# A start-up change in a one-core attention-plus-MLP kernel: constant idle products, V units split in two, earlier wk transposes, tile 0 transposed on TensorE

## Chip, cores, metric

The kernel runs on one core of a Trainium2 chip. The metric is the device time of one execution in microseconds (us). Single executions spread by about 1 us here, so medians, ranges and ratios over several runs are given, always with runs of the kernel before on the same chip.

## The reference, cut to what matters

```python
def reference(A_x, A_wqkv, A_w_phi, A_wo, B_x, B_w1, B_w3, B_w2):
    # x: 1 x 2048 x 640 bf16; 32 heads of 20; MLP width 1536
    xn = _layernorm(x)
    # A: q, k, v = xn @ wqkv; per head phi(q), phi(k) = softmaxes of +-(. @ w_phi);
    #    linear attention with kv = phi(k)^T v and z = sum phi(k); then @ wo
    # B: (silu(xn @ w1) * (xn @ w3)) @ w2
    return x + A(xn) + B(xn)
```

Three facts matter. Everything needs the normalised tokens transposed (xnT). V of the first 512 tokens is computed from centred tokens (xcT), with the scale applied at the eviction, so that it can start early. The feature matrix is folded into the key weights ("fold1": Wkp = wk @ w_phi, block by block). That needs wk transposed, which the DMA does while loading.

## The kernel before

The program lists operations with their dependencies. A planner at build time orders them per engine with estimated durations and seeded random tie-breaking. Then waits are put in. Where TensorE has nothing to do in the first 12 us, the planner inserts idle products ("filler"), which keep the array active. The parts that the change touches:

```python
memset("DVE", zero[:], 0.0, 9)                       # operand of the idle products
...
def filler(t, until):
    while t < until:
        cold = t < 5.2
        n = 512 if until - t > 0.5 else 128
        c = n / (1200 if cold else 2400)
        # emits matmul(bank, zero[:, 0:128], zero[:, 0:n])
        P.all.pop().raw = set(zeroed)                # waits for the memset
...
def v_pair(t, level):        # V0 and V1 in one unit of four PSUM banks
    both = P.begin(4, level, stream="V")
    for a, b, u in ((0, 3, 0), (0, 3, 1), (3, DC, 0), (3, DC, 1)):
        ...                  # chunks 0-2 of V0, of V1, then chunks 3-4 of each
...
load_x(0, 1, lv); ...; on_act(2.65, load_x, 3, 4)    # token tiles 0..3
load_w13(0, 384, lv - 4)                             # w1, w3: columns for 3 MLP units
first = [P.all[n]]                                   # the first of these two loads
for e in range(DC):
    o = load_wT(1, e, lv - 9 - e, first)             # transposes of wk wait for it
...
TURNED = (0,)                                        # tile 0 of xnT by DMA transpose
```

An "MLP unit" is five products of 128x512 with w1 and five with w3. Only three such units can run on the first weight loads.

The softmax here doesn't subtract the row's maximum and nothing guards it: scores larger than these inputs give would overflow.

## Time and profile before

| | before |
|---|---|
| median of the first 3 runs | 274.41 us (274.11 to 274.45) |
| span of the profiled run | 272.6 us |
| TensorE busy | 268.8 us, 99% |
| idle products | 4.84 us of the chain |
| first MLP weight load / first fold weight load | 14.01 / 20.40 us |

In the chain of waits a line has its start, its length and what ran. In a timeline a line has start, length, engine, operation and count, with the idle time ahead of it and its releaser in square brackets. PE is TensorE and PEld its weight loads, DVE VectorE, ACT ScalarE, POOL GpSimd; SPq and ACTq are the queues of SyncE and ScalarE, from which loads are issued. Ends of products are modelled, so I use starts and the spacing of starts.

### The profile page before, as it was taken

What the parts mean: (1) busy time and instruction counts of PE and PEld (TensorE: products, weight loads), DVE (VectorE), ACT (ScalarE), POOL (GpSimd) and SP (SyncE); (2) the same over time, 40 slices, a digit from 0 to 9 for tenths busy, and PEclk for the clock granted to TensorE, in tenths of its full rate; (3) what the DMA queues carried; (4) which work ended last, traced back from release to release, by engine and by line L of the source; (5) the groups of instructions that cost most, each with busy time, mean ns of one, the idle gap of its engine ahead of it and who ended that gap; (6) DMA issues with size and microseconds to landing.
All of it is one profiled execution on the core that took longest, in us unless ns stands there. A gap on an engine that the chain in (4) does not pass through costs nothing.

```text
span 272.6 us, 5091 instructions
## 1 busy us (share of the span) xinstructions
PE 268.8 (99%) x2099; PEld 159.9 (59%) x2099; DVE 183.8 (67%) x326; ACT 104.2 (38%) x193; POOL 60.5 (22%) x101
## 2 busy tenths in 40 slices
PE   8999999999999999999999999999999999999996
PEld 4747446777754448444444446677677774444774
DVE  5748998999999443588969795677673215666112
ACT  5637754776754540356663354100110002222000
POOL 3320552689999900000000000000000000000000
PEclk9999999999999999999999999999999999999999
DMA  7968996763000000803111111433353222000001
GB/s 233 183 95 258 345 216 129 118 175 114 2 0 2 0 0 10 284 1 46 29 26 24 24 26 25 98 100 96 90 107 83 64 75 72 0 0 0 26 24 48
DMA packets 41959, 22.14 MB, mean 81 GB/s; under 512 B 27728, under 2 KB 41936, under 8 KB 41936
## 3 DMA queue, kind: packets, MB, share of 16 engines
q1 hardware_dynamic: 41360, 21.17, 32.6%
q10 hardware_dynamic: 576, 0.66, 0.7%
q8 instruction: 16, 0.26, 0.4%
q14 instruction: 7, 0.06, 0.1%
HBM read 12.81 MB, written 2.62 MB: 57 GB/s over the span
## 4 chain that ended last, share of the span: by engine, by line
PE 99%; DVE 0%; issue 0%
PE PS L620 96%; PE PS L1094 2%; PE PS L811 1%; PE PS L865 0%; DVE xres L628 0%; DVE zero L628 0%; DVE warm L628 0%
## 5 line engine op out<-in xcount | busy, mean ns | idle before, releaser
L620 PE MATMUL PS<-xnT,w_s 128*128 128x512 bf16 x480 | 106.7, 379 | 0.0
L620 PEld LDWEIGHTS PS<-xnT,w_s 128*128 128x128 bf16 x480 | 46.6, 98 | 55.2
L620 PE MATMUL PS<-w_s,hT 128*128 128x320 bf16 (+2 forms) x384 | 55.0, 300 | 0.0
L628 ACT ACTIVATE th<-PS 128x512 f32<-128x512 f32 x48 | 28.7, 597 | 68.8 <-PE PS L620 68.8
L628 DVE SCALAR_TENSOR_TENSOR t<-th,PS 128x512 bf16<-128x512 f32 x48 | 32.7, 684 | 29.8 <-ACT th L628 29.8
L620 PEld LDWEIGHTS PS<-w_s,hT 128*128 128x128 bf16 x384 | 36.9, 98 | 14.8
L628 POOL TENSOR_TENSOR ekt<-ekt,rS 128x640 bf16<-128x640 bf16 x32 | 39.4, 1268 | 0.7 <-DVE rS L628 0.7
L628 DVE TENSOR_TENSOR xres<-PS,xres 128x640 bf16<-128x640 f32 (+2 forms) x17 | 13.4, 786 | 36.9 <-PE PS L620 36.9
L628 DVE SCALAR_TENSOR_TENSOR hT<-t,PS 128x512 bf16<-128x512 bf16 x48 | 32.7, 683 | 1.3
L628 ACT ACTIVATE EqT<-PS 128x512 bf16<-128x512 f32 x40 | 21.8, 594 | 11.3 <-PE PS L620 11.3
L628 ACT ACTIVATE e_s<-PS 128x64 f32<-128x64 f32 x32 | 9.1, 283 | 40.6 <-PE PS L620 40.1
L620 PE MATMUL PS<-wo_s,oT 128*128 128x320 bf16 (+2 forms) x160 | 24.5, 299 | 0.0
L628 DVE TENSOR_TENSOR prod<-PS,g_s 128x1280 bf16<-128x1280 f32 x16 | 23.9, 1492 | 0.6
L620 PE MATMUL PS<-Wkp,xnT 128*128 128x320 bf16 x160 | 23.9, 299 | 0.0
L628 ACT ACTIVATE ekt<-PS 128x640 bf16<-128x640 f32 x32 | 20.7, 698 | 7.5 <-PE PS L620 7.3
L620 PE MATMUL PS<-xnT,Wqp 128*128 128x512 bf16 x100 | 23.4, 380 | 0.0
L628 DVE TENSOR_REDUCE S<-ekt 128x64 f32<-128x1280 bf16 x16 | 22.9, 1449 | 0.0
L620 PEld LDWEIGHTS PS<-wo_s,oT 128*128 128x128 bf16 x160 | 15.7, 98 | 6.1
L620 PEld LDWEIGHTS PS<-Wkp,xnT 128*128 128x128 bf16 x160 | 15.5, 98 | 5.9
L620 PE MATMUL PS<-wv,xnT 128*128 128x320 bf16 x120 | 18.3, 299 | 0.0
L628 DVE BATCH_NORM_STATS2 bst<-x_tok 128x6 f32<-128x320 bf16 x32 | 13.9, 464 | 2.9 <-DMA x_tok<-in_A_x_dram 2.9
L620 PEld LDWEIGHTS PS<-xnT,Wqp 128*128 128x128 bf16 x100 | 9.3, 98 | 10.8
(68 smaller groups left out, 171.0 us busy)
## 6 DMA issues: line engine op xcount, KB each, us to landing
w_s<-in_B_w_dram SPq DMA_DIRECT2D x8, 480.0 KB, 7.7
xres<-in_A_x_dram SPq DMA_DIRECT2D x16, 160.0 KB, 2.2
out_dram<-xres SPq DMA_DIRECT2D x15, 160.0 KB, 1.8
x_tok<-in_A_x_dram SPq DMA_DIRECT2D x3, 640.0 KB, 7.5
w_s<-in_B_w_dram SPq DMA_DIRECT2D x1, 1920.0 KB, 9.1
wo_s<-in_A_wo_dram SPq DMA_DIRECT2D x1, 800.0 KB, 4.7
x_tok<-in_A_x_dram SPq DMA_DIRECT2D x2, 160.0 KB, 3.4
x_tok<-in_A_x_dram ACTq DMA_DIRECT2D x2, 160.0 KB, 3.8
```

Of the source, the lines that this page charges most:

```text
L620: return nc.tensor.matmul(o(u.k), l, r, start=start, stop=stop, skip_group_check=shared)
L628: return getattr(e, name)(*[at(a, u) for a in args], **{k: at(v, u) for k, v in kw.items()})
L811: return nc.tensor.transpose(PSb[:, a:a + 128], l, ident[:])
L1094: return nc.tensor.matmul(bank(u.k, n), zero[:, 0:128], zero[:, 0:n], start=True, stop=True)
```

## The change

It is meant to shorten the start: no memset and no wait ahead of the idle products, less of them, V0 able to start without tile 1, wk transposed sooner, and one DMA transpose less on the queue.

```diff
-TURNED = (0,)
-SEED = 385
+TURNED = ()
+SEED = 817
...
-        memset("DVE", zero[:], 0.0, 9)
-        zeroed.append(P.all[-1])
...
-    def v_pair(t, level):
+    def v_split(t, level, later, cut):
+        u = P.begin(2, level)                      # chunks 0..2
+        ...
+                P.begin(0, later).name = f"V{t}b"  # chunks 3..4, same banks, later
+                P.unit.anchor = u
...
+    ones = nc.const_aps.tensor(1.0, [128, 512], bf)
...
-            n = 512 if until - t > 0.5 else 128
-            c = n / (1200 if cold else 2400)
+            n = 512 if until - t > 0.9 else 128
+            c = n / (1200 if t < 6.5 else 2400)
...
-                return nc.tensor.matmul(bank(u.k, n), zero[:, 0:128], zero[:, 0:n], ...)
+                return nc.tensor.matmul(bank(u.k, n), ones[:, 0:128], ones[:, 0:n], ...)
...
-    on_act(2.65, load_x, 3, 4)
+    third = on_act(2.65, load_x, 3, 4)
...
-    first = [P.all[n]]
+    first = [third]
...
-    v_pair(0, 6e4)
+    v_split(0, 6e4 + 20, 6e4 - 8, 3)
+    v_split(1, 6e4 - 5, 6e4 - 9, 3)
...
-    P.schedule({"PE": 1.25, ...}, filler, 12.0, SEED, 175.0)
+    P.schedule({"PE": 0.8, ...}, filler, 12.0, SEED, 175.0)
```

More of the change, by code (lines that the diff above doesn't have):

```diff
@@ L573, in bass_parallel_sum__linear_kernel_hedgehog__glu_gated_swiglu__prompt_kernel @@
     hT1 = new("hT1", [128, FC, 512], bf, RH + 12288)
-    zero = new("zero", [128, 512], bf, RH + 12288)
     RE = region(40960)
@@ L723, in load_wT @@
                     A_wqkv[:, which * D + 128 * e:which * D + 128 * e + 128], level, True, after)
-    zeroed = []
     def consts():
         memset("DVE", warm[:], 0.0, 19)
-        memset("DVE", zero[:], 0.0, 9)
-        zeroed.append(P.all[-1])
         add([w_act(warm[:], warm[:], ACT.Exp, 8)], [warm[:]], [warm[:]], None, 3e9)
@@ L791, in centre @@
         o, i, z = xc[:, t, :], x_tok[:, t, :], mv[:, t, 6:7]
-        if by == "ACT":
-            add([way("ACT", "activation", (junk[:], i, ACT.Copy), dict(scale=-1.0 / D, accum_out=z), 0.86, 0.92)],
+        if by == "BOTH":
+            h, zb = D // 2, mv[:, t, 7:8]
+            add([way("ACT", "activation", (junk[:, 0:h], i[:, 0:h], ACT.Copy), dict(scale=-1.0 / D, accum_out=z),
+                     0.55, 0.58)], [junk[:, 0:h], z], [i[:, 0:h]], None, level)
+            add([way("DVE", "tensor_scalar", (junk[:, h:D], i[:, h:D], -1.0 / D, None, ALU.mult, ALU.add),
+                     dict(accum_out=zb), 0.48, 0.52)], [junk[:, h:D], zb], [i[:, h:D]], None, level)
+            add([w_op("DVE", "tensor_scalar", (o, i, z, zb, ALU.add, ALU.add), 0.31, 0.41)], [o], [i, z, zb], None,
+                level)
+        elif by == "ACT":
+            add([way("ACT", "activation", (junk[:], i, ACT.Copy), dict(scale=-1.0 / D, accum_out=z), 0.86, 0.87)],
                 [junk[:], z], [i], None, level)
-            add([w_op("DVE", "tensor_scalar", (o, i, z, None, ALU.add), 0.35, 0.44),
+            add([w_op("DVE", "tensor_scalar", (o, i, z, None, ALU.add), 0.31, 0.41),
                  w_act(o, i, ACT.Identity, D, 1.0, z)], [o], [i, z], None, level)
@@ L798, in centre @@
             m = mv[:, t, 0:1]
-            add([w_op("DVE", "tensor_scalar", (o, i, m, None, ALU.subtract), 0.35, 0.44)], [o], [i, m], None, level)
+            add([w_op("DVE", "tensor_scalar", (o, i, m, None, ALU.subtract), 0.31, 0.41)], [o], [i, m], None, level)
     def xc_transpose(t, level):
@@ L831, in v_first, with src @@
             [v2[:, t, 0:672]], [r], [0, 1], 1e6)
-    def v_pair(t, level):
-        both = P.begin(4, level, stream="V")
-        both.name = f"V{t}+"
-        for a, b, u in ((0, 3, 0), (0, 3, 1), (3, DC, 0), (3, DC, 1)):
-            if b == DC and u == 1:
-                P.begin(0, level - 30, stream="V").name = f"V{t + 1}"
-                P.unit.anchor = both
+    def v_split(t, level, later, cut):
+        u = P.begin(2, level)
+        u.name = f"V{t}a"
+        for a, b in ((0, cut), (cut, DC)):
+            if a:
+                P.begin(0, later).name = f"V{t}b"
+                P.unit.anchor = u
             for i in range(a, b):
                 for q in range(2):
-                    mm(2 * u + q, lambda k, q=q, u=u: bank(k + 2 * u + q, 320), xcT[:, t + u, i, :],
-                       wv[:, i, 320 * q:320 * q + 320], i == 0, i == DC - 1)
-            if b == DC:
-                o = v2[:, t + u, 0:672].rearrange("p (b h c) -> p b h c", b=2, c=21)[:, :, :, 0:DH]
-                r = mv[:, t + u, 4:5]
-                def src(k, u=u):
-                    return bank2(k + 2 * u, 320).rearrange("p b (h c) -> p b h c", c=DH)
-                last = P.unit.mms[-1]
-                P.unit = both
-                add([w_act(o, src, ACT.Copy, D, r),
-                     w_op("DVE", "tensor_scalar", (o, src, r, None, ALU.mult), 0.74, 0.83)],
-                    [v2[:, t + u, 0:672]], [r], [2 * u, 2 * u + 1], 1e6, [last])
+                    mm(q, lambda k, q=q: bank(k + q, 320), xcT[:, t, i, :], wv[:, i, 320 * q:320 * q + 320],
+                       i == 0, i == DC - 1)
+        P.unit.mms[0].war.add(u.mms[-1])
+        o = v2[:, t, 0:672].rearrange("p (b h c) -> p b h c", b=2, c=21)[:, :, :, 0:DH]
+        r = mv[:, t, 4:5]
+        def src(k):
+            return bank2(k, 320).rearrange("p b (h c) -> p b h c", c=DH)
+        last = P.unit.mms[-1]
+        P.unit = u
+        add([w_act(o, src, ACT.Copy, D, r), w_op("DVE", "tensor_scalar", (o, src, r, None, ALU.mult), 0.74, 0.83)],
+            [v2[:, t, 0:672]], [r], [0, 1], 1e6, [last])
     def xn_transpose(t, level):
@@ L1089, in filler @@
         while t < until:
-            cold = t < 5.2
-            n = 512 if until - t > 0.5 else 128
-            c = n / (1200 if cold else 2400)
+            n = 512 if until - t > 0.9 else 128
+            c = n / (1200 if t < 6.5 else 2400)
             def emit(n=n):
-                return nc.tensor.matmul(bank(u.k, n), zero[:, 0:128], zero[:, 0:n], start=True, stop=True)
+                return nc.tensor.matmul(bank(u.k, n), ones[:, 0:128], ones[:, 0:n], start=True, stop=True)
             P.mm(emit, [], 0, c, n)
-            P.all.pop().raw = set(zeroed)
+            P.all.pop()
             t += c
@@ L1209, in bass_parallel_sum__linear_kernel_hedgehog__glu_gated_swiglu__prompt_kernel @@
         out_tile(t, when(200 + 5 * t))
-    P.schedule({"PE": 1.25, "ACT": 1.12, "DVE": 0.93, "POOL": 0.8, "SP": 0.81}, filler, 12.0, SEED, 175.0)
+    P.schedule({"PE": 0.8, "ACT": 1.12, "DVE": 0.93, "POOL": 0.8, "SP": 0.81}, filler, 12.0, SEED, 175.0)
     lists = P.emit(finish)
```

## The prediction

> **What bounds the kernel now.** I read the page first: busy shares, slices, and the chain that ended last.
>
> ```profile
> PE 268.8 (99%) x2099; PEld 159.9 (59%) x2099; DVE 183.8 (67%) x326; ACT 104.2 (38%) x193; POOL 60.5 (22%) x101
> ...
> PE   8999999999999999999999999999999999999996
> ...
> PE 99%; DVE 0%; issue 0%
> PE PS L620 96%; PE PS L1094 2%; PE PS L811 1%; PE PS L865 0%; DVE xres L628 0%; DVE zero L628 0%; DVE warm L628 0%
> ```
>
> TensorE has no hole between the first slice and the last, and the chain is TensorE for 99% of the span. The next engine, VectorE, is at 67%. So a change to loads, evictions or their order pays only where TensorE does something other than work of the reference: the idle products (line 1094), which fill its waits at the start, and products run before its clock is up. The chain in order of time (start, length, what) says how much that is:
>
> ```profile
> 0.96 0.28 DVE zero L628
> ...
> 1.29 3.60 PE PS L1094 x11
> 4.88 0.54 PE PS L811 x5
> 5.42 0.74 PE PS L1094 x4
> 6.16 0.53 PE PS L811 x5
> 6.70 2.45 PE PS L620 x16
> 9.15 0.28 PE PS L811 x5
> 9.43 0.54 PE PS L620 x4
> 9.97 0.50 PE PS L1094 x9
> 10.47 1.36 PE PS L620 x10
> 11.83 0.28 PE PS L811 x5
> 12.11 0.84 PE PS L865 x15
> 12.95 119.14 PE PS L620 x945
> ...
> 270.13 0.42 DVE xres L628
> ```
>
> Idle products take 3.60 + 0.74 + 0.50 = 4.84 us. The last real product ends at 270.13, so the useful stream is 270.13 - 1.29 - 4.84 = 264.00 us, and after 12.95 us nothing but useful products is left (two pieces of 0.01 us apart). Five transposes take 0.54 and 0.53 us early on and 0.28 later; sixteen value products take 2.45 us where ten take 1.36 later, which would be 2.18. The slow clock therefore costs 0.26 + 0.25 + 0.27 = 0.78 us of useful work. Everything a perfect start could give back is the 1.24 us of idle products after 4.88, this 0.78, and what the arrival of token tile 0 allows before that (0.2 us at most, below).
>
> The view of the tile of idle operands and that of the normalised-token transposes show the clock in single durations (ns, min/median/max), the view of VectorE's timeline when tile 0 is centred, and TensorE's waits that nothing but the start makes it wait:
>
> ```profile
> L1094 PE MATMUL PS<-zero x24: 219/314/634, 1.3 to 10.3; 128*128 128x128 bf16 x16, 128*128 128x512 bf16 x8
> ```
> ```profile
> 4.03 0.39 DVE L628 TENSOR_SCALAR xc<-x_tok,mv 128x640 bf16<-128x640 bf16 x1
> ...
> 4.89 0.39 DVE L628 TENSOR_SCALAR xc<-x_tok,mv 128x640 bf16<-128x640 bf16 x1
> ```
> ```profile
> PE PS L1094 <- DVE zero L628: 1.3, 1, 1.3
> ```
>
> A 128x128 product lasts 314 ns cold and 219 warm. Tile 0 is centred at 4.42 and its transposes start at 4.68; tile 1 at 5.28, but its transposes start only at 5.96, behind idle products that were issued for a later arrival than came.
>
> **What the Trainium skill says.** "TensorE: Matmul & The Clock Gate", Part 1 (the HAM clock gate): the array starts at half clock, and one window of about 3.4 us of sustained activity, free-running against the kernel, releases it. The trace agrees on the two rates: from start to start the idle 128x512 products are 427 ns apart until the change and products of that width 216 ns apart later. The change falls at about 7.1 us, inside the value products (267 ns apart, one of 193, then 136), 5.8 us after the first product. The page's PEclk row shows 1.00 from the start and hides it. Same page, Part 4 (PE-mode transpose): a transpose lasts some 275 ns in a kernel; here the median over the first twenty is 267 ns, but their spacing is 56 ns warm, which is what counts in a stream. "Perfetto Trace Analysis", Identifying the Most-Contended Engine: matmul busy time is a poor measure of distance to the roofline. That warning holds for single durations (379 ns against 216 ns of spacing), so I count with pieces of the chain instead. "DMA: Bandwidth & Descriptors", Issuing engines are not separate DMA queues: all queues share the 16 engines. The trace fits: the two weight loads issued at 4.68 and 5.11 land at 10.66 and 12.16, and the transpose of tile 0, issued behind them at 6.52, at 12.88.
>
> **The change part by part.**
> (1) Idle products from a constant. The zero tile (a 0.27 us memset on VectorE, and TensorE's wait for it until 1.29) goes. The constant is written by 0.47 us, before the common start, so idle products can begin at about 0.85. This moves no useful product: tile 0 lands at 3.15, the sum on ScalarE and the centring end at 4.42. It gives the clock 0.44 us more of activity. If its release follows the first product, it comes at 6.7 instead of 7.1, and 0.44 us less useful work runs at half rate: -0.2. If the window's edges stand where they are, nothing. I take -0.1.
> (2) The idle stretches are cut anew (wide ones only above 0.9 us, half rate assumed until 6.5 us, costs of centring lowered to what is measured). First transposes at about 4.5 for 4.68: -0.15. Between tile 0's and tile 1's transposes, data allow 5.35: of the 0.74 us of idle products about 0.3 stay: -0.45.
> (3) V0 and V1 in two units each instead of one four-bank unit. The product count is the same (20 + 20). V0's first three chunks need only tile 0, so they can run from about 5.9, when its transpose is evicted (5.94 before), instead of 6.49. By then a few more useful products run cold: +0.1. V0's last two chunks need the weights landing at about 7.0. Summed in order: V0a 5.9 to 7.3, V1a to 8.1, V0b and V1b to 9.2.
> (4) Tile 0's normalised tokens transposed on TensorE: five more transposes, 0.28 us by the row above, and one more eviction of 0.49 us on VectorE or 0.70 on ScalarE. They are ready at about 6.5 (normalised by 6.49) and fit where 0.50 us of idle products stood at 9.97: they replace idle time rather than add to it. Of the 0.50 I leave 0.2 standing, since tile 2 is not centred before 8.58 and must still be transposed and evicted: -0.30 +0.28. On the queue it frees 1.31 us of issue.
> (5) Transposes of wk behind tile 3 (landing at 7.28) rather than the first weight load (10.66): issued about 3.4 us earlier, so the folded key weights come some 3 us before 20.6, and the token loads behind them at about 17 instead of 20.5. TensorE has MLP work throughout, so this is worth nothing in the sum; it only gives slack.
> (6) The new seed reorders units up to 175 us. The work is equal and there is no gap to win. Switches into and out of the row mode cost about 0.1 us each and their number is fixed by the sixteen query tiles. I take 0 +- 0.2.
>
> Sum: -0.1 -0.15 -0.45 +0.1 -0.30 +0.28 = -0.62 us. From 274.41 this is 273.8.
>
> **The rivals.**
> A: the clock decides. Over 0.31 to 3.73 (one window back from the two edges that the change at 7.14 implies) TensorE was busy from 1.29, 71%; from 0.85 it would be 84%. If that suffices, the clock is up at 3.73, no useful product is cold, and 0.78 us more goes: about 273.0. Against: that window is not full, and the edges may stand elsewhere in each run; the spread of three runs (274.11 to 274.45) is the size of such a shift.
> B: a new wait in place of the filler. With idle products cut short, tile 2's centring (8.19 to 8.58, after ScalarE's sum) or the weights at 7.0 to 7.3 would hold V2 at 10.3 just the same; the idle time moves, and the five transposes are added in full: 274.3 to 274.6. For: ScalarE handles tile 2's sum only at 7.33. Against: tile 2 landed near 5.05, so the order can be better.
> C: the earlier wk transposes hold back the weight loads needed by the first MLP unit at 14.14. Ring order puts them behind, and the loads land at 12.16 before, so 1 to 1.5 us of delay would be needed to hurt: up to +1, unlikely.
> D: the new order opens a stall in the middle (VectorE is 80% busy or more in slices 4 to 13). Each tenth of a slice is 0.7 us; nothing in the diff adds more than one eviction, so I give over 1 us one chance in fifteen.
>
> **Range and chances.** The centre of the sum is 273.8; A weighs more than C and D together, so I put 273.7. Low end: most of A, 273.0. High end: B, 274.5. Two per cent is 5.5 us. Only 4.84 us of idle products plus 0.78 us of slow clock exist, and 3.6 of that lie before tile 0 can be there, so faster by 2% cannot come from this stage: 0.01. Slower needs a 5.5 us stall on an engine now never waiting: 0.01. Within 2%: 0.98.
>
> **What would show it.** Idle products from about 0.85, still until about 4.5 (1 right); fewer than 0.8 us of them after 4.6 (2, 4); tile 1's transposes before 5.6 and value products before 6.2 (2, 3); twenty normalised-token transposes; first MLP product near 13.5 for 14.14; wk transposes issued at 7.3 to 7.8 (5). From there on the stream should be the old one moved by 0.5 to 0.8 us, ending near 269.5 for 270.13. Wrong if TensorE shows a wait after 13 us, if the first MLP product waits for a weight load, if the clock comes up more than 1 us away from 7, or if the gain at 13 us is gone again at 175.

## The result, and the profile after

A ratio is the mean time of one kernel's runs over that of the other's of the same rounds, so it is not quite the ratio of the medians quoted.

| rounds | changed, median (range) | before, median (range) | ratio, 95% interval |
|---|---|---|---|
| first | 274.21 (273.51 to 274.48), 6 runs | 274.32 (273.46 to 274.52), 6 runs | 0.9998, 0.9981 to 1.0016 |
| with e5, another chip | 273.74 (273.52 to 274.45), 6 runs | 274.85 (273.54 to 276.07), 11 runs | 0.9969, 0.9941 to 0.9997 |
| with e10, another chip | 273.93 (273.23 to 274.66), 6 runs | 274.25 (273.61 to 275.58), 11 runs | 0.9979, 0.9958 to 0.9999 |

The differences of the means are -0.05, -0.81 and -0.50 us, -0.45 us on average, for the -0.62 us of the prediction's sum. It is the same within 2%, as predicted. The first rounds alone show no gain at all. The page of the changed kernel, busy shares and the engines of the chain:

```profile
PE 267.5 (98%) x2082; PEld 159.9 (59%) x2101; DVE 180.8 (66%) x322; ACT 106.0 (39%) x197; POOL 61.1 (22%) x101
...
PE 92%; DMA 3%; SPq 3%; issue 1%; ACTq 0%; ACT 0%; DVE 0%
```

Two things are to be seen. There are 2101 weight loads but 2082 matmuls: 19 records of matmuls are missing. Each leaves a hole of one product (216 ns for 128x512), and "0.05 issue" in the chain below is such a hole and no wait. Before comparing busy times of two traces, compare these two counts. What is real is that the chain no longer is all TensorE. In order of time:

```profile
2.36 4.85 DMA x_tok<-in_A_x_dram
...
7.22 1.22 SPq L693
...
8.49 2.37 SPq L693
...
15.22 3.49 DMA wqkT<-in_A_wqkv_dram
18.71 0.14 issue
18.85 9.07 PE PS L619 x75
27.92 0.05 issue
```

The end now hangs on the load of token tile 3, the transposes of wk issued behind it (line 693) and the landing of the last one at 18.71. At that instant TensorE stands in the first fold, as the timeline shows:

```profile
18.05 0.42 PE L619 MATMUL PS<-BDc,wqkT 128*128 128x140 bf16 x5
...
18.85 0.85 PE L619 MATMUL PS<-BDc,wqkT 128*128 128x140 bf16 x13 [0.38 <-DMA wqkT<-in_A_wqkv_dram]
```

The fifth product starts at 18.25 and the sixth at 18.85 where 0.06 is usual: a wait of 0.54 us. (The brackets say 0.38 because the end of the fifth is modelled.) The kernel before ran thirty MLP products ahead of the folds and went through them without a wait:

```profile
20.62 1.82 PE L620 MATMUL PS<-BDc,wqkT 128*128 128x140 bf16 x30
```

The changed kernel runs only twenty first. Its head start is there: the first MLP weight load is at 13.61 for 14.01, 0.40 us earlier. Then the fold wait takes 0.54 away, other differences of the plan give 0.16 back, and the last product starts at 269.81 for 269.83. The start itself, by TensorE's timeline of the changed kernel:

```profile
0.84 4.00 PE L1098 MATMUL PS<-const-bfloat16-1.0 128*128 128x512 bf16 x15 [0.84 <-PEq L1263]
...
4.63 0.74 PE L814 MATMUL PS<-ident,xc 128*128 128x128 bf16 x5
...
5.17 0.84 PE L1098 MATMUL PS<-const-bfloat16-1.0 128*128 128x128 bf16 x6
...
5.96 1.23 PE L619 MATMUL PS<-wv,xcT 128*128 128x320 bf16 x6
```

Idle products from 0.85, first value products at 5.96 for 6.49, idle products and waits of 0.79 us after the first transposes, and a wait of 0.14 at 8.1 us, for 1.25 together.

### The profile page after: what moved, and what is told of

The parts are those of the page before. It is cut to its first block, busy times and chain, and to the rows that moved or that the text cites. A ratio compares the mean times of both kernels' runs of the same rounds, so it can differ in the third digit from the quotient of the medians.

```text
span 272.6 us, 5074 instructions
## 1 busy us (share of the span) xinstructions
PE 267.5 (98%) x2082; PEld 159.9 (59%) x2101; DVE 180.8 (66%) x322; ACT 106.0 (39%) x197; POOL 61.1 (22%) x101
## 4 chain that ended last, share of the span: by engine, by line
PE 92%; DMA 3%; SPq 3%; issue 1%; ACTq 0%; ACT 0%; DVE 0%
PE PS L619 92%; SPq L693 3%; DMA x_tok<-in_A_x_dram 2%; DMA wqkT<-in_A_wqkv_dram 1%; ACTq L689 0%; SPq L689 0%; ACT L627 0%; DVE xres L627 0%
## 5 line engine op out<-in xcount | busy, mean ns | idle before, releaser
L619 PE MATMUL PS<-xnT,w_s 128*128 128x512 bf16 x464 | 105.4, 379 | 0.9 <-issue 0.2
```

Of the source, the lines that this page charges most:

```text
L619: return nc.tensor.matmul(o(u.k), l, r, start=start, stop=stop, skip_group_check=shared)
```

## The experiments

The theory to test: the head start is real but is given back at the first fold, because the planner moves the fold ahead to where it believes wk has landed. Rival 1: the visible wait is not worth its length in the end. Rival 2: the instant at which the array's clock comes up, which differs from run to run, decides.

### e1 to e4: edits through the planner

Four edits, each of one line or rule, and the planner run again:

```diff
# e1, on the changed kernel
+    third_mlp = next(u for u in P.units if u.name == "M0.2")
+    for u in P.units:
+        if u.name.startswith("fold1."):
+            u.behind.append(third_mlp.mms[-1])
# e2, on the changed kernel
-    first = [third]
+    first = [P.all[n]]
# e3, on the kernel before: idle products from ones as in the change, PE 0.8
# e4, on the kernel before
-    first = [P.all[n]]
+    first = [third]
```

> The changed kernel, with one rule added: the units that fold the feature matrices into wk come after the third MLP unit (30 MLP products), as they stood in the kernel before, and not after the second (20). Theory: the changed kernel won about 0.4 us up to the first MLP product and lost 0.54 us of it at 18.3 us, where the first fold waited for the last transpose of wk, landing at 18.7. Then here the folds start at about 20.3 with no wait, the last product starts 0.5 us earlier than in the changed kernel (269.3 for 269.8), and the time is 273.7 for 274.2. Rival 1: the wait is only the visible part of a lost slack, and something later (evictions on VectorE) gives the same end: last product at 269.8, time 274.2. Rival 2: the times are set by when the array's clock comes up, which differs from run to run: then profile and time move with that instant and not with the wait.

> The changed kernel with the wk transposes again behind the first weight load (undoes that part alone). The order on TensorE still has the first fold after 20 MLP products. Theory (the wait at the fold is on the path): the last transpose of wk lands near 20.5 us, the first fold is reached at about 18.2 and waits 2.2 to 2.4 us, the time is 1.6 to 1.9 us above the changed kernel's, about 276.0. Rival 1 (a wait there is made up later): time within 0.3 us of 274.2, no wait of more than 0.6 us at the fold.

> The kernel before with idle products from the constant alone (and TensorE's start in the plan at 0.8). Folds stay after 30 MLP products. Theory of the head start: idle products from 0.85 us, first transposes at 4.6 as before, nine narrow idle products at 9.8 become four; first MLP product 0.1 to 0.4 us before 14.14, time 274.0 to 274.2. Rival 2 (the clock comes up with the first product): the clock's change moves 0.4 us to 6.7, another 0.2 us is won, 273.8.

> The kernel before with the wk transposes behind token tile 3 alone. The plan then puts the first fold after 20 MLP products here too. Theory: first MLP product unchanged at 14.1, fold reached at 18.5, last wk transpose lands at 18.6 to 19.2, a wait of 0.2 to 0.7 us, time 274.5 to 274.9: this part alone is a loss. What the prediction said (worth nothing, slack only): no wait, 274.3.

| run | median (range) | ratio to before (274.20), interval |
|---|---|---|
| e1 | 274.68 (274.48 to 275.10) | 1.0014, 0.9993 to 1.0036 |
| e2 | 278.40 (275.29 to 278.74) | 1.0126, 1.0081 to 1.0172 |
| e3 | 275.87 (274.68 to 277.78) | 1.0066, 1.0026 to 1.0106 |
| e4 | 274.81 (274.49 to 276.38) | 1.0032, 1.0000 to 1.0064 |

These four mostly missed, and for a reason worth knowing. One changed dependency makes the seeded planner draw another plan. In e2, e3 and e4 it put the transposes of one token tile directly ahead of the first MLP unit, which then waited for their eviction: starts 1.03, 1.24 and 1.03 us apart where 0.06 is usual. In e1 the first value weights landed at 6.57 us (4.96 in the changed kernel), and value products waited 0.94 us. None of the four isolates what it was meant to. Nor does e4 show its expected fold wait: wk had landed by then. e2 waited 0.69 us at its fold where 2.2 to 2.4 were expected, since wk landed at 19.32. And e2, with wk late, runs twenty MLP products ahead of the fold just as e4 does with wk early. So it is not shown that the earlier issue is what made the planner move the fold.

Two things do come out. Three of the four timed runs of e2 and one of e3 had a mean granted clock of 0.994 and spans of 276.0 to 277.0 us: 0.006 x 277 = 1.7 us lost, as much as 3.3 us at half rate cost. So longer waits early in the program may cost more than themselves. No trace caught such a run, so this is not shown, and which wait would do it stays open. And the instant of full clock in the traces ranged from 4.04 us (e2) to some point between 5.8 and 6.7 us (e1, in a wait).

### e5 to e8: the plan kept

From here on the planner runs unaltered, and the edit is made in its finished plan. Banks and waits are then derived again, so instructions other than the edited ones keep their order.

```diff
# e5: the changed kernel itself
# e6: changed kernel, after P.schedule(...)
+    # move the ten products of M0.2 and its three evictions ahead of the first fold, on each engine;
+    # recompute which evictions each unit's banks wait for
# e7: changed kernel, after P.schedule(...)
+    for o in wk_loads:
+        o.raw.discard(third)
+        o.raw.add(first_w1)
# e8: kernel before, after P.schedule(...)
+    for o in wk_loads:
+        o.raw.discard(first_w1)
+        o.raw.add(third)
```

> The changed kernel itself, for more runs and a second trace. Theory (clock phase): the array's clock comes up anywhere between about 4.0 and 7.4 us (the five traces of kernels that start idle products at 0.85 have 4.0, 5.9, 6.5 and 6.7 so far), spans of 271.8 to 273.4 as before; the wait at the first fold stands at 0.3 to 1 us whatever the clock does. Time 273.5 to 274.7, median 274.2.

> The changed kernel with its plan kept instruction for instruction, except that the third MLP unit (10 products and its three evictions) stands ahead of the first fold, as in the kernel before. Theory: the fold is reached near 20.2 us, after wk has landed (18 to 19), no wait at the fold; everything behind is shifted by 0.5 us or what the wait of the same chip's changed kernel is: median 0.4 to 0.7 us below the changed kernel of the same rounds, about 273.6. Rival 1: same median as the changed kernel within 0.2 us. (The earlier try with a rule in the planner reshuffled the plan after 20 us and had its value weights late, so it could not tell.)

> The changed kernel with its plan kept, wk transposes behind the first weight load again: one wait moved, no instruction moved. Theory: last wk transpose lands at 20 to 21 us, the fold is reached at 18 and waits 2 to 2.7 us; span 1.7 to 2.2 us longer than the changed kernel in its profile. If the array's clock drops because of that wait, the mean clock shows 0.994[...] and another 1.7 us goes. Rival 1: no more than 0.3 us longer.

> The kernel before with its plan kept (first fold after 30 MLP products, at 20.4), wk transposes behind token tile 3. Theory: transposes land near 18.7 and nobody waits for them at 20.4, so the end does not move: 274.2, within 0.2 us of the kernel before of the same rounds. If the early transposes hold back the first weight load so that the first MLP product starts later than 14.14 by more than 0.2 us, the prediction's rival C has a part in it, and the time is 274.5 or more.

| run | median (range) | ratio to before (274.85), interval |
|---|---|---|
| e5 | 273.74 (273.52 to 274.45) | 0.9969, 0.9941 to 0.9997 |
| e6 | 274.62 (274.46 to 275.12) | 1.0000, 0.9973 to 1.0027 |
| e7 | 275.44 (274.63 to 277.85) | 1.0055, 1.0006 to 1.0105 |
| e8 | 273.59 (273.46 to 274.26) | 0.9965, 0.9937 to 0.9993 |

e5 is as expected in time, and its trace is instructive: the clock was up at 4.61, and yet the first MLP load came only at 14.02, later than in the first trace of the changed kernel (clock at 6.48, load at 13.61). The chain of its first 15 us says why:

```profile
1.73 5.27 DMA x_tok<-in_A_x_dram
...
7.94 0.40 DVE xc L627
...
8.39 0.45 PE PS L814 x5
8.84 2.72 PE PS L619 x20
```

Token tile 2 landed at 7.00 us (5.61 in the first trace), and its transposes started at 8.39, as soon as it was centred. The value weights were late too, as the view of their tile shows (idle time before its products, us and times, by releaser):

```profile
  DMA wv<-in_A_wqkv_dram: 0.9, 2
  ACT xcT L627: 0.6, 2
```

Their fourth and fifth chunk landed at 7.23 and 7.84 us (6.71 and 6.90 in the first trace), and TensorE stopped for them in V0's second unit. But the last product of that unit started at 8.03 and takes 0.14 us, so tile 2 was the later by about 0.2 us: it is the wait that counts. All ten products of V1 stand behind the transposes of tile 2 in the plan, so nothing could fill either wait. An early clock is worth little while tokens and weights are not there.

e7, the same plan with wk later, shows the fold wait grown to 1.18 us:

```profile
17.71 0.42 PE L619 MATMUL PS<-BDc,wqkT 128*128 128x140 bf16 x5
...
19.15 0.85 PE L619 MATMUL PS<-BDc,wqkT 128*128 128x140 bf16 x13 [1.02 <-DMA wqkT<-in_A_wqkv_dram]
```

It was less than the 2 to 2.7 us expected, because wk landed at 19.02. Its profiled run is 0.8 us shorter than the median of its runs, so in most of them the wait was probably longer; one has the 0.994 clock. Its direction speaks against rival 1.

e6 failed as a removal. Its fold no longer waited for wk, but the moved unit sat in banks still being read. Its products paused for 0.50 us, and the folds paused about another 0.35 us behind the moved evictions. I had traded one wait for two others.

e8 was a surprise. It was expected to be worth nothing, since in the trace of the kernel before nobody waits for wk. It is 0.92 us faster in the mean than the kernel before, and its runs stay between 273.46 and 274.26 where those of the kernel before go up to 276.07. In the trace of the kernel before the last transpose of wk lands at 20.47, and the sixth fold product, the first to read it (as the waits above show), starts at 20.87. The margin there is 0.40 us, less the 0.14 that the chain above shows between landing and product. In e8 it lands at 19.53. This suggests that the kernel before waits at its folds in its slower runs. e3, another plan of the kernel before with wk behind the same load and thirty MLP products first, shows such a wait in its trace: 0.50 us, with the last landing at 22.15.

### e9 to e12

```diff
# e9: as e6, but M0.2 takes banks 4-5 and fold1.0, fold1.3 take 6-7 as in the kernel before;
#     the last eviction of M0.2 stays behind the copies of the folded weights
# e10: the changed kernel itself
# e11: kernel before, after P.schedule(...)
+    for o in wk_loads:
+        o.raw.discard(first_w1)
+        o.raw.add(second_w)            # the load of w3, behind that of w1
# e12: changed kernel, after P.schedule(...)
+    P.ops = [o for o in P.ops if o.eng != "PE" or o.unit in P.units]   # no idle products
```

> As e6, mended: the changed kernel's plan with the third MLP unit ahead of the first fold, now in the banks that the kernel before gives it and the folds, and with the last eviction of that unit left behind the copies of the folded weights (e6 had put the unit into a bank still being read, a wait of 0.5 us, and its evictions ahead of the folds', another 0.35). Theory: no wait at the fold (reached near 20.2, wk landed by 17.6 to 18.9), so from the first MLP product to the last product start it is 255.7 us, as in the changed kernel without its fold wait (255.66 in all three traces). Median 0.3 to 0.6 us below the changed kernel of the same rounds. Rival 1: within 0.2 us of it.

> The changed kernel beside e9 on the same chip, with a third trace. Theory: last product start minus first MLP load is 255.66 us plus the wait at the first fold, to 0.1 us, whatever the clock and the arrivals did before; median 273.6 to 274.3, e9's 0.3 to 0.6 below it.

> The kernel before, plan kept, wk transposes behind the second of the first two weight loads (landing at 12.2 for 10.7), so about 1.5 us later. Theory: the kernel before had no slack at its fold (last wk transpose at 20.47, the product that reads it at about 20.6), so the delay comes out in full: last transpose at 21.7 to 22.2, a wait of 1.1 to 1.7 us, time 1.2 to 2 us above before, 275.5 to 276.5 (3 us where the clock drops). If the kernel before had slack of more than 1 us there, as the prediction took it, the time stays at 274.2 to 274.8.

> The changed kernel without any idle products; everything else kept. Theory: TensorE starts at about 4.6 us cold, its clock comes up[...] between 8 and 12 us or not before the first unbroken stretch; useful work of 3.5 to 7 us runs at half rate, which costs 1.7 to 3.5 us, less the 0.4 to 0.9 us of arrival waits that a slower stream hides: time 275.3 to 277. If the idle products hardly matter (the arrivals decide), within 0.5 us of 274.2.

| run | median (range) | ratio to before (274.25), interval |
|---|---|---|
| e9 | 273.90 (273.65 to 274.46) | 0.9978, 0.9959 to 0.9996 |
| e10 | 273.93 (273.23 to 274.66) | 0.9979, 0.9958 to 0.9999 |
| e11 | 275.53 (274.55 to 275.75) | 1.0028, 1.0003 to 1.0053 |
| e12 | 275.05 (274.54 to 275.27) | 1.0020, 0.9995 to 1.0046 |

e10 gives the trace of a good run of the changed kernel, with no record missing. wk had landed at 16.39, the fold never waits, and the chain is TensorE again from 5.57 on:

```profile
5.03 0.50 ACT xcT L627
...
5.57 0.99 PE PS L619 x6
6.56 0.28 PE PS L814 x5
...
12.00 118.38 PE PS L619 x925
...
141.37 127.62 PE PS L619 x999
```

e11 shows that the kernel before had little slack: wk 1.3 us later (last landing at 21.73) gives two waits in the fold, starts 1.09 and 0.75 us apart.

```profile
19.87 0.36 PE L620 MATMUL PS<-BDc,wqkT 128*128 128x140 bf16 x4
...
21.11 0.22 PE L620 MATMUL PS<-BDc,wqkT 128*128 128x140 bf16 x1 [0.89 <-DMA wqkT<-in_A_wqkv_dram]
...
21.86 1.31 PE L620 MATMUL PS<-BDc,wqkT 128*128 128x140 bf16 x20 [0.53 <-DMA wqkT<-in_A_wqkv_dram]
```

The median rises by 1.28 us (the mean by 0.86), at the low end of what was expected. The waits are 1.74 us in all, though wk was only 1.26 us later than in the trace of the kernel before, because the folds were reached 0.75 us sooner. Had wk landed at 20.47 here, a wait of about 0.5 us would have been left (an estimate from the two traces).

All traces with an intact plan side by side, in us. The fold wait is the excess of the spacing of starts over the usual one. "Rest" is the last product's start less the first MLP weight load less the fold wait.

| trace | clock up | first MLP load | fold wait | last product | rest |
|---|---|---|---|---|---|
| before | 7.14 | 14.01 | 0 | 269.83 | 255.82 |
| e8 (before, wk earlier) | 7.01 | 13.95 | 0 | 269.76 | 255.81 |
| e11 (before, wk later) | 3.98 | 13.27 | 1.74 | 270.82 | 255.81 |
| changed | 6.48 | 13.61 | 0.54 | 269.81 | 255.66 |
| e5 (changed) | 4.61 | 14.02 | 0.28 | 269.95 | 255.65 |
| e10 (changed) | about 4.2 | 13.07 | 0 | 268.71 | 255.64 |
| e7 (changed, wk later) | 5.02 | 13.27 | 1.18 | 270.11 | 255.66 |
| e12 (changed, no idle products) | 8.21 | 14.40 | 0 | 270.05 | 255.65 |

The rest is constant to 0.02 us for each plan while the fold wait goes from 0 to 1.74. So the fold wait counts in full, microsecond for microsecond, and rival 1 falls. The changed plan itself is 0.16 us shorter after the first MLP load. Rival 2 has a part: with the head of the kernel before, the first MLP load is 0.7 us earlier with the clock at 3.98 than at 7.0 to 7.1. But it doesn't decide alone, as e5 shows.

e9 is the mended removal: no wait for wk, but about 0.25 us on evictions within the folds, and last product less first MLP load is 255.95 instead of the 255.7 expected. Its median is that of e10 within 0.03 us, so the expected 0.3 to 0.6 us did not come. On that chip the changed kernel's fold wait can have been small; in the one trace it was zero. The intervals are too wide to say more.

e12 tells what idle products are worth. Without them the clock comes up at 8.21 us, and the first six value products run at half rate:

```profile
4.64 0.72 PE L814 MATMUL PS<-ident,xc 128*128 128x128 bf16 x5 [4.64 <-DVE xc L627]
5.93 1.78 PE L619 MATMUL PS<-wv,xcT 128*128 128x320 bf16 x6 [0.58 <-ACT xcT L627]
```

Six value products take 1.78 us of this timeline where the changed kernel's six took 1.23. The median is 1.1 us above e10's. That is less than the 1.4 us or more that I had expected: a stream that starts cold also meets fewer late weights.

No version beats both kernels beyond doubt. e8, which takes one line of the change, equals the changed kernel on the same chip (273.59 and 273.74).

## Why the prediction was right or wrong, point by point

It was right in its class and range, and its central size is near the mean of the three comparisons, which go from -0.05 to -0.81 us. That is partly luck: the sum left out two terms of opposite sign, the wait at the folds of the changed kernel (0 to 0.54 us) and what an earlier wk spares the kernel before (e8: -0.92 us in the mean). The ways to the number were partly wrong.

- Step 1 (constant): idle products began at 0.85 as stated, and nothing useful moved by itself. The clock came up between 3.59 (e6) and at most 6.7 us (e1) in traces of kernels that start there, 3.98 to 7.14 in kernels that start at 1.29. Rival A's early clock does happen, in some runs of either kernel.
- Steps 2 and 3 (idle stretches, V in two units): in the first trace they worked nearly as told: transposes at 4.64, first value products at 5.96, V and all transposes done at 13.6 for 14.0. That is -0.40 for a sum of -0.62. Tile 1's transposes came at 7.02 rather than before 5.6, because the planner put V0's products first. The term that was mis-sized is what the idle products hide. With an early clock the landings of tile 2 (5.6 to 7.0 us by the run) and of the last value weights (6.9 to 7.8) set the pace, and cutting idle products wins little. And the split has a price: the planner put V0's second unit and the transposes of tile 2 ahead of all of V1, so ten value products stand before those transposes where the kernel before has sixteen. With an early clock and tile 2 late (landing at 6.90 and 7.00) the transposes of tile 2 start at 8.23 in the kernel before (e11) and at 8.39 in the changed one (e5). The latter then has six more value products to run, 0.82 us, and the first MLP load is at 14.02 for 13.27. With tile 2 at 6.03 (e10) the changed head got there at 13.07. That the order of the units makes this difference is read from the waits of these traces; no run tested it alone.
- Step 4 (tile 0 on TensorE): twenty transposes instead of fifteen, 0.28 us more, and no idle products behind 6 us in the trace. As told.
- Step 5 (wk earlier) is the step that failed: "worth nothing in the sum; it only gives slack". wk was issued at 7.22 instead of 10.68, as said. But the kernel before had a margin of 0.40 us at most at its folds, so earlier wk has a value in its slower runs (e8: -0.92 us in the mean). In the plan of the changed kernel the slack was then spent (e2 leaves open whether for this reason): the first fold comes after twenty MLP products instead of thirty, at 17.84 for 20.40, while the last landing moved only from 20.47 to 18.72. So a wait of 0 to 0.54 us stands there in its three traces. The prediction's own test, a wait of TensorE after 13 us, is what showed it.
- Step 6 (seed): 0 was said; -0.16 us is measured in the part behind the first MLP load, fold wait taken off. That is seed and all other differences of the plan together.
- Rival B: the prediction took 5.05 us for tile 2's landing. The waits of the later traces show that this was the third weight chunk and that tile 2 landed at 6.15. In the first trace of the changed kernel it did no harm: tile 2 landed at 5.61 and its sum began at 5.80. In e5 it landed at 7.00, and its centring held TensorE until 8.39, as the rival feared.
- Rival C (wk holding back the weight loads) did not happen: the second weight load landed at 12.74 for 12.16 in the first pair, but between 11.0 and 13.1 over the changed kernel's traces, and no first MLP unit waited for it with the plan intact.
- Two readings of the prediction say less than it took from them. The 267 ns for a transpose is only the middle between ten cold (314) and ten warm ones (219). The three loads that it names for the shared DMA engines were all issued by SyncE, so they don't test what loads of different issuers do to each other.

What stays open: no slow run of the kernel before was traced. Of its 39 runs 13 lie above 274.6 us, of the changed kernel's 18 one. That those are fold waits is concluded from e8 and e11 and not seen. Also open is which wait brings the 0.994 clock.

## What to carry to other kernels

A wait that is absent in one trace can be 0.3 us away from being there: look at the margin between a landing and its first reader, not only at the waits. When a planner works on estimated landings, slack that one edit gives can be spent by the plan of the next build, so compare the order of instructions along with the times. To test one dependency, keep the plan and alter it alone, then add up in each trace a stretch that should be constant.

## What the Trainium skill lacked or had wrong

- "TensorE: Matmul & The Clock Gate", Part 1, puts the release of the clock at about 4 us of sustained activity, give or take 0.5, with a free-running window of 3.4 us. Over the fourteen traces the full rate came 2.7 to 5.9 us after the first product. With windows of that length, counted back from the change (no trace shows their edges, so this is an estimate), one in which TensorE was busy 80% of the time released it in e6, 79% in e11 and 77% in e12, and one of 71% did not (the kernel before). The page gives no such share.
- The same page, Part 4, says that transposes don't bring the array to full rate and last some 275 ns in a kernel. Here they lasted 311 to 315 ns cold and 219 ns warm, 107 and 56 ns apart: once other products have released the clock, transposes run at the full rate. And they seem to count as activity: without them the window of e12 is 51% busy, less than the 71% that did not suffice.
- "DMA: Bandwidth & Descriptors", DMA Transpose (X-bar), gives no time from issue to landing for a small one (a table elsewhere on the page has only cycles of the sequencer). Five loads of 128x640 with transposition, issued behind other loads, were 1.2 to 3.1 us each on the issuing queue (3.1 in e8) and landed 2.8 to 7.1 us after issue, and the last of them moved from 16.4 to 18.9 us over three traces of one kernel.
- No page that I used says that matmul records can be missing from a trace: 19 of 2101 in that of the changed kernel, none in e10's. Comparing the count of matmuls with that of weight loads shows it.
